# A DMA queue's estimate counts all transfers; a batch's first x + h is put 12 places sooner and cast at once, and block turns wait until its turn is given out

## The chip, the cores and the metric

The kernel runs on one core of a Trainium2 chip. The metric is the device time of one execution in microseconds (us). A core has TensorE (PE, matmuls, with weight loads shown as PEld), VectorE (DVE), ScalarE (ACT), GpSimd (POOL) and SyncE (SP). Here SyncE issues every transfer, in one order; SPq in a row of the trace is that queue.

## The reference

Eight batches, 3136 positions, width 256. An attention without a softmax gates u; its result goes through a mixer of low rank and a two-layer channel part. All inputs and the output are float32.

```python
scores = scale * np.matmul(z, z.transpose(0, 2, 1))      # z: 8 x 3136 x 64, scale = 1 / 3136
attn = np.maximum(scores, 0.0) ** 2
x = u * np.matmul(attn, v)                               # u, v: 8 x 3136 x 256
h = x.transpose(0, 2, 1) @ U @ V                         # U: 3136 x 32, V: 32 x 3136
y = x + h.transpose(0, 2, 1)
ch = np.maximum(y @ w_ch1, 0.0) @ w_ch2                  # 256 -> 1024 -> 256
out = y + ch
```

## The kernel before, in words

**Tiles and stages.** The positions of a batch are cut into 7 groups: six of 512 (groups 0 to 5, four tiles of 128 each) and a last one of 64 (group 6). One pair (batch, group) is an item, and the 56 items are worked off one after the other. During item t the kernel runs the attention-value product (AV) of item t, makes scores for coming items, and finishes the mixer and the channel part of items 7 and 8 places back, that is, of the batch before. All operands of matmuls are bfloat16. Matmuls mostly come in pairs that use the upper and the lower 64 rows of the array at once (`pair`, line 159, whose matmul is line 164; most rows of PE in the trace have that line).

**Blocks.** The score matrix of a batch is symmetric. A block `blk` holds the scores of 512 keys by 512 positions after scale, ReLU (lines 321 and 325) and square (line 315). Where block (J, g) is made and (g, J) is wanted too, it is not computed again: `issue_turn` (line 336) turns it with a DMA transpose on SyncE (line 341) into another block. There are 112 such block turns, and 20 blocks to hold everything. `take_block` and `give_block` hand blocks out first come, first served. A turn becomes ready 7 units after its square; it is then appended to `ready_turns`. The block it reads can't be given back before it is issued.

**The chain from x to ch1.** `av_out` (line 588) writes x = u * AV as bfloat16 (`x_bf`, line 592). When all groups of a batch are there, `t1_all` (line 630) multiplies with U on PE, and DVE finishes the small result `t_sb` (lines 648 and 649). For each group, `u2_unit` (line 661) multiplies V with `t_sb` in four matmuls (rows `ps<-t_sb,V_bf`), and DVE adds x (line 708) into `out_sb` in float32. A cast (`cast`, line 181; rows of line 186 on DVE or 184 on ACT) writes it over `x_bf`, and `x_turn` (line 621) turns it with a DMA transpose (line 624) into `u2T`. The first matmuls of `ch1_part` (line 753) read `u2T`; `ch2_stream` and `ch2_out` make the output. This document calls the result of `u2_unit` "x + h" and the transfer of line 624 the "x turn".

**What sets the order.** The order of all instructions is written out by the Python program ahead of time, with an estimated clock. `clock[0]` counts the matmuls given out so far, in units of a pair's 256 columns (`pe`, line 121). `free_at` holds for ACT, DVE and SP the estimated time at which each is free; `book` (line 102) adds a cost. `hold(due, f)` puts off a step until the clock reaches its due time, and `run_held` (line 109) runs what is due, and then issues ready block turns as long as SP is free by the estimate. In the kernel before, the only entry for SP is 34 units for each block turn (line 345): loads, outputs, x turns and turns of z are not counted.

`emit` (line 857) walks along a light stream (AV or ch2, one unit a place) and puts the other units in at given places: each queue entry is (place, PSUM buffers needed, whether the way of the AV rows turns, unit). An entry that needs a buffer waits up to 14 places beyond its own, or 4 for entries that turn the way in some items, until one is free by the estimate (`ps_ready`, line 171). The x + h of an item's batch before is put in at line 1179.

**Waits on the chip.** SyncE's instructions run in the listed order; each waits for the semaphores of its source, of its target's last readers and of earlier transfers. What is listed behind a waiting transfer waits with it.

Of the kernel before, what the change touches and what calls it, by code (L numbers as in the profile page):

```python
# [18 lines left out]
def kernel(  # L19
# [11 lines left out]
    nc = tc.nc  # L31
# [5 lines left out]
    P = 128  # L37
# [60 lines left out]
    held = []  # L98
    unturned = {}
    ready_turns = []  # L100

    def book(eng, ready, cost):
        free_at[eng] = max(free_at[eng], ready) + cost
        return free_at[eng]

    def hold(due, f):
        held.append((due, len(held), f))

    def run_held(now=None):
        now = clock[0] if now is None else now  # L110
        while True:
            ripe = [h for h in held if h[0] <= now]
            if not ripe:
                break
            h = min(ripe, key=lambda e: (e[0], e[1]))
            held.remove(h)
            h[2]()
        while ready_turns and free_at["sp"] <= now:
            issue_turn(min(ready_turns, key=lambda e: (e[0], e[2], e[1])))

    def pe(cost):
# [75 lines left out]
    def load_tail(raw, c0, a, n):  # L197

        for h in range(2):
            nc.sync.dma_start(out=raw[h * TAIL : (h + 1) * TAIL, c0 : c0 + n], in_=a[NF * P : S, :])  # L200


    def load_z_piece(b, t0, n, raw, tail=True):
        m = min(n, NF - t0)
        nc.sync.dma_start(  # L205
            out=raw[:, : m * dqk].rearrange("p (t d) -> p t d", d=dqk), in_=rows_of(z[b])[:, t0 : t0 + m, :]
        )
        if n > m and tail:
            load_tail(raw, m * dqk, z[b], dqk)
            load_tail(raw, n * dqk, v[b], D)  # L210
# [15 lines left out]
    def load_v_piece(b, k, raw):  # L226
        nc.sync.dma_start(
            out=raw.rearrange("p (t d) -> p t d", d=D), in_=rows_of(v[b])[:, k * GT : (k + 1) * GT, :]
        )

    def v_copy(b, k, raw, copy):
        copy(out=v_bfs[b][:, k * GT : (k + 1) * GT, :], in_=raw.rearrange("p (t d) -> p t d", d=D))
# [41 lines left out]
    def load_u(b, g):  # L274
        g0, gw = groups[g]
        t = pool.tile([P, GT, D], FP32, name="u_sb", bufs=2)
        if gw >= P:
            nc.sync.dma_start(
                out=t[:, : gw // P, :],
                in_=rows_of(u[b])[:, g0 // P : (g0 + gw) // P, :],  # L280
            )
        else:
            nc.sync.dma_start(out=t[:gw, 0, :], in_=u[b, g0 : g0 + gw, :])
        u_sbs[b, g] = t


    def z_turn_dma(b):
        nc.sync.dma_start_transpose(
            out=zzTs[b], in_=z_bfs[b].rearrange("p t c d -> p (t c d)")
        )  # L290

    def z_turn(b, t0, copy):
        n = min(2 * GT, NT - t0)
# [327 lines left out]
    def x_turn(b, g, turned):  # L621
        n = len(tiles_of(g))
        rows = min(P, groups[g][1])
        nc.sync.dma_start_transpose(
            out=turned[:, :n, :, :rows].rearrange("p q d c -> p (q d) c"),
            in_=xs[b, g][:rows, :n, :].rearrange("p q d -> p (q d)"),
        )


    def t1_all(b):  # L630
# [30 lines left out]
    def u2_unit(b, g, turn=True):  # L661
        ts = tiles_of(g)
        n, t0, rows = len(ts), ts[0][1], ts[0][2]
        k, ps = take_ps()
        if n == GT:
            for a in range(2):
                pair(
                    k,
                    crossed(
                        0,  # L670
                        a,
                        lambda h, q: dict(
                            out=four(ps)[:, q, :],
                            lhsT=V4_bf[h, (t0 + q) * P : (t0 + q + 1) * P],
                            rhs=t1s[b][h, :],
                            start=(a == 0),
                            stop=(a == 1),
                        ),
                    ),
                    D,  # L680
                )
        else:
            pair(
                k,
                [
                    (
                        0,
                        0,
                        dict(
                            out=ps[:, 0, :D],  # L690
                            lhsT=V4_bf[:hp, t0 * P : (t0 + 1) * P],
                            rhs=t1s[b][:hp, :],
                            start=True,
                            stop=True,
                        ),
                    )
                ],
                D,
            )
        x = xs[b, g][:rows, :n, :]  # L700
        if b == B - 1:
            entry, raw = stage_block()
            o_blocks[b, g] = entry
            o = raw.rearrange("p (q d) -> p q d", d=D)
        else:
            o = pool.tile([P, GT, D], FP32, name="out_sb", bufs=3)
        done = ps_free[k] = book("dve", clock[0] + 3, 11.2 * n / GT)
        nc.vector.tensor_tensor(out=o[:rows, :n, :], in0=four(ps)[:rows, :n, :], in1=x, op=ALU.add)  # L708
        u2s[b, g] = o
        if not turn:  # L710
            return

        def turned():
            u2Ts[b, g] = u2T_tile()
            x_turn(b, g, u2Ts[b, g])

        def down():
            hold(cast(x, o[:rows, :n, :], n * D) + 2, turned)

        hold(done - 3, down)  # L720


    def u2T_unit(b, g):
# [99 lines left out]
    def ch2_out(b, g, acc):  # L823

        for e in relus.pop((b, g)):
            give_block(e)
        ts = tiles_of(g)
        n, t0, rows = len(ts), ts[0][1], ts[0][2]
        o = u2s.pop((b, g))[:rows, :n, :]
        nc.vector.tensor_tensor(out=o, in0=acc, in1=o, op=ALU.add)  # L830
        dst = rows_of(out[b])[:, t0 : t0 + n, :] if rows == P else out[b, t0 * P : S, None, :]
        nc.sync.dma_start(out=dst, in_=o)
        if (b, g) in o_blocks:
            give_block(o_blocks.pop((b, g)))

# [80 lines left out]
    def load_U():  # L916
        entry, raw = stage_block()
        nc.sync.dma_start(out=raw[:, : NF * R].rearrange("p (t r) -> p t r", r=R), in_=rows_of(moe_U))
        nc.sync.dma_start(out=raw[:TAIL, NF * R : NT * R], in_=moe_U[NF * P :, :])

        def casts():
            cast(U_bf[:, :NF, :], raw[:, : NF * R].rearrange("p (t r) -> p t r", r=R), NF * R)
            cast(U_bf[:TAIL, NF, :], raw[:TAIL, NF * R : NT * R], 100)
            give_block(entry)

        return [casts]

    def load_w(k):
        def step(i):
            entry, raw = stage_block()  # L930
            if k == 0:
                nc.sync.dma_start(out=raw, in_=moe_w_ch1[i * P : (i + 1) * P, :])
                dst = w1_bf[:, i, :]
            else:
                nc.sync.dma_start(
                    out=raw.rearrange("p (t d) -> p t d", d=D),
                    in_=moe_w_ch2.rearrange("(t p) d -> p t d", p=P)[:, i * GT : (i + 1) * GT, :],
                )
                dst = w2_bf[:, i * GT : (i + 1) * GT, :].rearrange("p t d -> p (t d)")

            def casts(entry=entry, raw=raw, dst=dst):
                cast(dst, raw, GT * D)
                give_block(entry)

            return [casts]

        return [lambda i=i: step(i) for i in range(2)]


    def load_V(i0):  # L950
        n = P // 4

        def step(i):
            entry, raw = stage_block()
            w = n * NF + (S - NF * P if i == 3 else 0)
            for c in range(NREP):
                nc.sync.dma_start(out=raw[c * R : (c + 1) * R, :w], in_=moe_V[:, i * n * NF : i * n * NF + w])

            def casts(i=i, entry=entry, raw=raw):
                cast(  # L960
                    V4_bf[:, : NF * P].rearrange("r (t p) -> r t p", p=P)[:, :, i * n : (i + 1) * n],
                    raw[:, : n * NF].rearrange("r (p t) -> r t p", t=NF),
                    2 * n * NF,
                )
                if i == 3:
                    nc.vector.memset(V4_bf[:, S:], 0.0)
                    cast(V4_bf[:, NF * P : S], raw[:, n * NF : n * NF + S - NF * P], 100)
                give_block(entry)

            return [casts]  # L970

        return [lambda i=i: step(i) for i in range(i0, i0 + 2)]
# [110 lines left out]
    for t in range(n_items):  # L1083
# [92 lines left out]
        if av and u2i:  # L1176
            if u2i[1] == 0:
                qm.append((8, 1, False, lambda: t1_all(u2i[0])))
            qm.append((34 if u2i[1] == 0 else 40, 1, False, lambda: u2_unit(*u2i)))

        if not av:
            qm += [(nC // 2, -1, False, small)] if nC else []
# [70 lines left out]
```

## Time and profile before

| what | value |
|---|---|
| median of 3 runs | 1010.28 us (1007.97 to 1010.57) |
| the profiled execution | 1010.08 us |
| its span, from the first to the last instruction | 1008.3 us |
| mean granted TensorE clock | 0.997 |
| DMA queue of SyncE | 165.59 MB, 76.3% of 16 engines' span |
| x turns (line 624) / block turns (line 341) / turns of z (line 288) | 56 / 112 / 7 |

How to read it: a row of the timeline has start and duration in us, engine, line, operation, out<-in, shapes and count; in brackets stands the idle time of the engine before it and who ended it. Rows of one engine that follow each other are merged. In a table of stretches each engine has its busy time and its number of instructions; then come the granted clock of TensorE (1.00 is full speed), the share of the DMA engines that is busy, and GB/s. Matmuls overlap, so the distance between starts tells their pace, not the duration of one.

### The profile page before, as it was taken

Reading aid. Unit: us, or ns where it says so; the run is one execution under the profiler, and the core shown is the slowest. Engines: PE = TensorE matmul, PEld = TensorE weight load, DVE = VectorE, ACT = ScalarE, POOL = GpSimd, SP = SyncE. Lnnn points to the kernel's source line nnn. Section 1 sums busy time; section 2 is a strip of 40 time slices with the busy share of each in tenths; the row PEclk is TensorE's granted clock in tenths of the full one; section 3 lists DMA queues with packets and bytes.
Section 4 is the critical chain, followed back from the end, with each engine's and each line's share of the span. In section 5 each row is a group of like instructions: output and inputs, shape, how many; then the busy total and the mean of one; then the engine's idle time right before and its main releaser. Section 6 shows DMA issues by size and latency. Waiting matters only on the chain.

```text
span 1008.3 us, 35337 instructions
## 1 busy us (share of the span) xinstructions
PE 986.7 (98%) x16179; PEld 784.7 (78%) x16179; DVE 653.6 (65%) x820; ACT 520.2 (52%) x599; POOL 17.2 (2%) x24
## 2 busy tenths in 40 slices
PE   6999899999999999999999999999999999999997
PEld 3898688877787777778777877778777777787776
DVE  5986675668666685666756677566776667653453
ACT  6896653357524573355733456444653356522453
POOL 4100000000000000000000000000000000000000
PEclk9999899999999999999999999999999999999999
DMA  7997998478966799568995789846798577873142
GB/s 247 187 257 178 235 170 166 130 166 186 213 142 165 152 199 218 149 145 181 182 209 157 129 193 188 210 127 140 179 216 185 137 158 143 160 127 88 45 103 94
DMA packets 337061, 167.84 MB, mean 166 GB/s; under 512 B 312336, under 2 KB 315408, under 8 KB 336912
## 3 DMA queue, kind: packets, MB, share of 16 engines
q1 hardware_dynamic: 336912, 165.59, 76.3%
q8 instruction: 126, 2.06, 0.8%
q14 instruction: 23, 0.19, 0.1%
HBM read 62.56 MB, written 25.69 MB: 88 GB/s over the span
## 4 chain that ended last, share of the span: by engine, by line
PE 94%; DVE 2%; ACT 2%; DMA 1%; issue 0%; POOL 0%; SPq 0%; POOLq 0%; ACTq 0%
PE ps L164 92%; PE ps L559 1%; DVE blk L315 1%; ACT blk L793 1%; PE ps L635 1%; DMA blk<-in_v_dram 1%; ACT blk L325 1%; PE ps L843 0%; DMA u2T<-x_bf 0%; DMA stage<-in_v_dram 0%; POOL z_bf L213 0%; SPq L205 0%; DVE blk L321 0%; DVE out_sb L708 0%; DVE blk L830 0%
## 5 line engine op out<-in xcount | busy, mean ns | idle before, releaser
L164 PEld LDWEIGHTS <-blk 64*128 64x128 bf16 x12288 | 617.6, 94 | 153.6 <-POOLq L154 8.7
L164 PE MATMUL ps<-v_bf,blk 64*128 64x256 bf16 x9216 | 617.2, 270 | 2.3 <-DVE blk L315 1.8
L325 ACT ACTIVATE blk<-ps 128x1024 bf16<-128x1024 f32 x324 | 323.4, 1027 | 337.2 <-PE ps L164 334.0
L315 DVE TENSOR_TENSOR blk<-blk 128x1024 bf16<-128x1024 bf16 x352 | 237.7, 701 | 34.1 <-ACT blk L325 33.4
L164 PE MATMUL ps<-u2T,w_bf 64*128 64x512 bf16 (+1 forms) x1792 | 239.1, 351 | 4.3 <-DMA u2T<-x_bf 3.5
L164 PE MATMUL ps<-w_bf,blk 64*128 64x256 bf16 x3072 | 193.7, 269 | 0.2
L790 DVE TENSOR_SCALAR blk<-ps 128x1024 bf16<-128x1024 f32 x96 | 115.7, 1205 | 102.3 <-PE ps L164 102.3
L793 ACT ACTIVATE blk<-ps 128x1024 bf16<-128x1024 f32 (+1 forms) x128 | 107.3, 847 | 82.4 <-PE ps L164 74.1
L164 PE MATMUL ps<-zzT 64*128 64x512 bf16 (+1 forms) x944 | 143.5, 342 | 1.9 <-ACT zzT L305 1.7
L164 PEld LDWEIGHTS <-w_bf 64*128 64x128 bf16 x1792 | 91.6, 94 | 35.1 <-DMA u2T<-x_bf 3.8
L592 DVE TENSOR_TENSOR x_bf<-ps,u_sb 128x1024 bf16<-128x1024 f32 x48 | 58.8, 1224 | 63.0 <-PE ps L164 62.9
L708 DVE TENSOR_TENSOR out_sb<-ps,x_bf 128x1024 f32<-128x1024 f32 (+1 forms) x49 | 54.3, 1107 | 53.7 <-PE ps L164 53.6
L830 DVE TENSOR_TENSOR out_sb<-ps,out_sb 128x1024 f32<-128x1024 f32 x42 | 51.3, 1222 | 18.3 <-PE ps L164 18.3
L164 PEld LDWEIGHTS <-zzT 64*128 64x128 bf16 x944 | 43.9, 95 | 9.2 <-ACT zzT L305 2.2
L325 ACT ACTIVATE last_sb<-ps 128x1024 bf16<-128x1024 f32 x23 | 23.5, 1024 | 26.5 <-PE ps L164 26.5
L321 DVE TENSOR_SCALAR blk<-ps 128x1024 bf16<-128x1024 f32 x24 | 29.4, 1224 | 10.3 <-PE ps L164 8.7
L186 DVE CAST x_bf<-out_sb 128x1024 bf16<-128x1024 f32 x33 | 22.8, 690 | 0.5
L186 DVE CAST v_bf<-stage 128x1024 bf16<-128x1024 f32 (+1 forms) x34 | 21.2, 626 | 0.0
L164 PE MATMUL ps<-t_sb,V_bf 64*128 64x256 bf16 x200 | 20.8, 269 | 0.0
L164 PE MATMUL ps<-v_bf,last_sb 64*128 64x256 bf16 x192 | 18.6, 269 | 0.0
L830 DVE TENSOR_TENSOR blk<-ps,blk 128x1024 f32<-128x1024 f32 x6 | 7.3, 1225 | 16.0 <-PE ps L164 15.9
L578 ACT COPY u_sb<-ps 64x512 f32<-64x512 f32 x8 | 4.7, 582 | 23.9 <-PE ps L559 23.9
(67 smaller groups left out, 249.5 us busy)
## 6 DMA issues: line engine op xcount, KB each, us to landing
u_sb<-in_u_dram SPq DMA_DIRECT2D x48, 512.0 KB, 5.0
stage<-in_v_dram SPq DMA_DIRECT2D x42, 512.0 KB, 6.0
out_dram<-out_sb SPq DMA_DIRECT2D x42, 512.0 KB, 3.1
stage<-in_z_dram SPq DMA_DIRECT2D x7, 512.0 KB, 5.5
blk<-in_v_dram SPq DMA_DIRECT2D x6, 512.0 KB, 7.2
out_dram<-blk SPq DMA_DIRECT2D x6, 512.0 KB, 2.6
blk<-in_moe_w_ch_dram SPq DMA_DIRECT2D x4, 512.0 KB, 5.8
stage<-in_z_dram SPq DMA_DIRECT2D x7, 256.0 KB, 5.7
```

Source lines behind the costliest of these rows:

```text
L164: ins = nc.tensor.matmul(**args)
L186: nc.vector.tensor_copy(out=out, in_=in_)
L315: nc.vector.tensor_tensor(out=a, in0=a, in1=a, op=ALU.mult)
L321: nc.vector.tensor_scalar(out=dst, in0=src, scalar1=scale, scalar2=0.0, op0=ALU.mult, op1=ALU.max)
L325: nc.scalar.activation(out=dst, in_=src, func=AF.Relu, scale=scale)
L559: nc.tensor.matmul(out=ps[c * hp : c * hp + rows, h, :D], lhsT=smalls[b][h * hp : (h + 1) * hp, jt, :], rhs=v_bfs[b][h * hp : (h + 1) * hp ...
L592: nc.vector.tensor_tensor(out=xs[b, g][:rows, :n, :], in0=four(box["ps"])[:rows, :n, :], in1=u_sbs[b, g][:rows, :n, :], op=ALU.mult,)
L635: nc.tensor.matmul(out=pt[c * R : (c + 1) * R, 0, :D], lhsT=U_bf[:rows, it, :], rhs=xs[b, g][:rows, q, :], start=(it < NREP), stop=(it + N ...
L708: nc.vector.tensor_tensor(out=o[:rows, :n, :], in0=four(ps)[:rows, :n, :], in1=x, op=ALU.add)
L790: nc.vector.tensor_single_scalar(out=r, in_=ps[:, :, :gw], scalar=0.0, op=ALU.max)
L793: nc.scalar.activation(out=r, in_=ps[:, :, :gw], func=AF.Relu)
L830: nc.vector.tensor_tensor(out=o, in0=acc, in1=o, op=ALU.add)
```

## The change

Four edits. First, a new function `queued` books SP's estimated time for every transfer by its size in KB: 15 units for 512 KB of plain transfer, 17 for 256 KB of an x turn or a turn of z. It is called behind each load, output, x turn and turn of z. The 34 units of a block turn stay. Second, `u2_unit` of a batch's first group (g == 0) does the cast on DVE at once behind the add, and holds the x turn until 6 units before the estimated end of that cast. Third, from that `u2_unit` until its x turn is given out, the list `urgent` is not empty, and `run_held` issues no ready block turn. Fourth, that `u2_unit` is due at place 22 of its item, not 34. (A block turn that AV needs at once would still be issued from `av_stream`; that code is not changed.)

```diff
+    urgent = []
...
+    def queued(kb, turned=False):
+
+        book("sp", clock[0], kb * (17 / 256 if turned else 15 / 512))
...
-        while ready_turns and free_at["sp"] <= now:
+        while ready_turns and free_at["sp"] <= now and not urgent:
             issue_turn(min(ready_turns, key=lambda e: (e[0], e[2], e[1])))
...
@@ load_tail, load_z_piece, load_v_piece, load_u, z_turn_dma, x_turn, ch2_out, load_U, load_w, load_V
+            queued(n / 4)                      (each of two small loads of the tail)
+        queued(m * dqk / 2)                    (z)
+        queued(GT * D / 2)                     (v; w_ch1, w_ch2)
+        queued(gw)                             (u)
+        queued(NT * P / 4, True)               (turn of z)
+        queued(n * D / 4, True)                (x turn)
+        queued(n * rows)                       (output)
+        queued(NF * R / 2)                     (U)
+                queued(w / 8)                  (each of four loads of V)
...
@@ u2_unit
         def turned():
             u2Ts[b, g] = u2T_tile()
             x_turn(b, g, u2Ts[b, g])
+            urgent.clear()
 
         def down():
             hold(cast(x, o[:rows, :n, :], n * D) + 2, turned)
 
-        hold(done - 3, down)
+        if g == 0:
+            urgent.append((b, g))
+            nc.vector.tensor_copy(out=x, in_=o[:rows, :n, :])
+            hold(book("dve", done, 6.3) - 6, turned)
+        else:
+            hold(done - 3, down)
...
-            qm.append((34 if u2i[1] == 0 else 40, 1, False, lambda: u2_unit(*u2i)))
+            qm.append((22 if u2i[1] == 0 else 40, 1, False, lambda: u2_unit(*u2i)))
```

More of the change, by code (lines that the diff above doesn't have):

```diff
@@ L200, in load_tail @@
             nc.sync.dma_start(out=raw[h * TAIL : (h + 1) * TAIL, c0 : c0 + n], in_=a[NF * P : S, :])
+            queued(n / 4)
     def load_z_piece(b, t0, n, raw, tail=True):
@@ L207, in load_z_piece @@
         )
+        queued(m * dqk / 2)
         if n > m and tail:
@@ L229, in load_v_piece @@
         )
+        queued(GT * D / 2)
     def v_copy(b, k, raw, copy):
@@ L283, in load_u @@
             nc.sync.dma_start(out=t[:gw, 0, :], in_=u[b, g0 : g0 + gw, :])
+        queued(gw)
         u_sbs[b, g] = t
@@ L290, in z_turn_dma @@
         )
+        queued(NT * P / 4, True)
     def z_turn(b, t0, copy):
@@ L627, in x_turn @@
         )
+        queued(n * D / 4, True)
     def t1_all(b):
@@ L832, in ch2_out @@
         nc.sync.dma_start(out=dst, in_=o)
+        queued(n * rows)
         if (b, g) in o_blocks:
@@ L919, in load_U @@
         nc.sync.dma_start(out=raw[:TAIL, NF * R : NT * R], in_=moe_U[NF * P :, :])
+        queued(NF * R / 2)
         def casts():
@@ L939, in step @@
                 dst = w2_bf[:, i * GT : (i + 1) * GT, :].rearrange("p t d -> p (t d)")
+            queued(GT * D / 2)
             def casts(entry=entry, raw=raw, dst=dst):
@@ L957, in step @@
                 nc.sync.dma_start(out=raw[c * R : (c + 1) * R, :w], in_=moe_V[:, i * n * NF : i * n * NF + w])
+                queued(w / 8)
             def casts(i=i, entry=entry, raw=raw):
```

## The prediction

> **What bounds the kernel now.** First the page of the profiled execution: its span, the engines' shares and the chain that ended last.
>
> ```profile
> span 1008.3 us, 35337 instructions
> PE 986.7 (98%) x16179; PEld 784.7 (78%) x16179; DVE 653.6 (65%) x820; ACT 520.2 (52%) x599; POOL 17.2 (2%) x24
> PE 94%; DVE 2%; ACT 2%; DMA 1%; issue 0%; POOL 0%; SPq 0%; POOLq 0%; ACTq 0%
> ```
>
> TensorE (PE) is the bound: it is busy 98% of the span and the chain runs through it for 94%. Only its idle time can be saved without taking matmuls out, and the change takes none out. So next comes the view of who waited for whom, for PE alone, over the whole span, and then the same view from 130 to 940 us.
>
> ```profile
> PE ps L296 <- ACT z_bf L213: 4.1, 1, 4.1
> PE ps L164 <- DMA u2T<-x_bf: 3.5, 1, 3.5
> PE ps L296 <- POOL z_bf L213: 3.4, 1, 3.4
> PE ps L164 <- DVE blk L315: 1.8, 2, 0.9
> ```
> ```profile
> PE ps L164 <- DVE out_sb L708: 0.2, 1, 0.2
> ```
>
> In the long middle, where six of the eight batches lie, PE waits 0.2 us in all: nothing can be won there. The waits on z_bf belong to the first 12 us, whose order is not touched. One wait touches the change: a single 3.5 us for `u2T`, the turned x + h. The timeline of PE places it in batch 0, at the first up-projection (ch1) of the whole kernel.
>
> ```profile
> 113.24 0.94 PE L164 MATMUL ps<-v_bf,blk 64*128 64x256 bf16 x14
> 114.01 0.40 PE L164 MATMUL ps<-v_bf,last_sb 64*128 64x256 bf16 x4
> 114.22 0.62 PE L164 MATMUL ps<-v_bf,blk 64*128 64x256 bf16 x8
> 118.38 1.04 PE L164 MATMUL ps<-u2T,w_bf 64*128 64x512 bf16 x4 [3.54 <-DMA u2T<-x_bf]
> ...
> 120.70 1.92 PE L164 MATMUL ps<-v_bf,blk 64*128 64x256 bf16 x16
> 122.41 0.64 PE L164 MATMUL ps<-zzT 64*128 64x512 bf16 x2
> ...
> 124.57 0.59 PE L164 MATMUL ps<-u2T,w_bf 64*128 64x512 bf16 x4
> ```
>
> The stall has a second part. Before it, 14 matmuls of 256 columns take 114.01 - 113.24 = 0.77 us, 0.055 us each; after it, 16 of the same kind take 122.41 - 120.70 = 1.71 us, 0.107 us each. The table of stretches says why, by its column PEclk (0.50, then 1.00):
>
> ```profile
> 118.30:124.40 6.10, 6.02 (x46) 3.43 (x48) 0.46 (x1) 3.27 (x4) 0.00 (x0) 0.50 1.01 254
> 124.40:130.00 5.60, 5.60 (x88) 4.10 (x85) 5.25 (x7) 3.79 (x6) 0.00 (x0) 1.00 1.11 163
> ```
>
> Behind the stall TensorE ran at half clock for some 6 us. Why u2T is late is seen on SyncE's queue (SP), which issues every transfer in order, beside VectorE (DVE), which makes what it turns:
>
> ```profile
> 105.26 2.76 SPq L341 DMA_TRANSPOSE blk<-blk  x1
> 108.06 1.05 SPq L278 DMA_DIRECT2D u_sb<-in_u_dram  x2
> 109.22 4.64 SPq L341 DMA_TRANSPOSE blk<-blk  x1
> 113.96 1.25 SPq L624 DMA_TRANSPOSE u2T<-x_bf  x1
> 115.32 3.35 SPq L341 DMA_TRANSPOSE blk<-blk  x1
> ```
> ```profile
> 102.61 0.22 DVE L649 COPY t_sb<-t_sb 64x256 bf16<-64x256 bf16 x1
> ...
> 103.48 0.69 DVE L315 TENSOR_TENSOR last_sb<-last_sb 128x1024 bf16<-128x1024 bf16 x1
> 104.08 1.29 DVE L315 TENSOR_TENSOR blk<-blk 128x1024 bf16<-128x1024 bf16 x2
> 105.47 1.22 DVE L708 TENSOR_TENSOR out_sb<-ps,x_bf 128x1024 f32<-128x1024 f32 x1
> 106.61 1.28 DVE L315 TENSOR_TENSOR blk<-blk 128x1024 bf16<-128x1024 bf16 x2
> 107.81 0.69 DVE L186 CAST x_bf<-out_sb 128x1024 bf16<-128x1024 f32 x1
> ```
>
> The cast was done at 107.81 + 0.69 = 108.5 us, but the turn was issued at 113.96: 5.5 us behind a queue in which two block turns held SP for 2.76 and 4.64 us.
>
> **The change part by part.** *The u2 unit sooner.* In the order in which the changed program lists its instructions, the x + h of batch 0's first group stands 22 matmuls sooner; in batches 1 to 6 it stands at the very same matmul as before, since the unit waits there for a free PSUM buffer whichever of the two places it is due at. In batch 0 it comes two matmuls into the first of these rows, instead of at the second:
>
> ```profile
> 103.63 1.25 PE L164 MATMUL ps<-v_bf,blk 64*128 64x256 bf16 x20
> ...
> 105.05 0.38 PE L164 MATMUL ps<-t_sb,V_bf 64*128 64x256 bf16 x4
> ```
>
> That is 103.63 + 2 x 0.055 = 103.74 us, 1.3 us sooner. Its operand t_sb is ready at 102.61 + 0.22 = 102.83, so the new place adds no wait. DVE still has squares queued; one fewer stands ahead of the add, so at their pace (0.6 us) the add L708 starts near 104.9 rather than 105.47.
>
> *The cast at once.* The add lasts 1.22 us and the cast 0.69: ready near 106.7, not 108.5. The two squares that stood between them come later. They are of scores whose turns are held back anyway, and no row shows PE waiting for a square in the window from 130 to 940 us. Without that cover a delay of 0.7 us is the most that one cast can put before a square. I take zero and keep 0 to 0.7 for each of seven batches, 0 to 5 us in all, with most of it near zero, since DVE is idle 35% of the span.
>
> *The fuller estimate and the turns held back.* No instruction is added: 112 block turns and 56 x + h turns remain, in another order. In the changed order, both block turns between the z loads and this x turn (the rows of 2.76 and 4.64 us) stand behind it, and there are three fewer in all since the w_ch2 loads. What stands ahead is the u loads (1.05 us), which follow PE's place and end near 107. So the x turn goes out at about 107. How long does it take to land? These are the view of u2T and the page's list of issues:
>
> ```profile
> DMA to landing us min/median/max: 2.3/3.3/5.4
> ```
> ```profile
> blk<-blk SPq DMA_TRANSPOSE x112, 5.2
> ```
>
> It lands between 107 + 3.3 = 110.3 and 107 + 5.4 = 112.4. ch1 needs it where the 8 matmuls from 114.22 end, 114.22 + 8 x 0.055 = 114.66. The margin is 2.3 to 4.4 us; at 118.38 it was nought. The stall is gone whole.
>
> What is late next: the block turns that step back. In the changed order, the smallest distance from a block turn's place to the matmul that reads it is 222 matmuls, 13 us by this run's clock (batch 0, block 5 for group 3), against 5.2 us for a turn to land; in batches 2 to 7 it is 25 us. No buffer is asked for sooner, and a turn takes its target block later, so more blocks are free. The next x turn, group 1 in each batch, has little margin. For batch 1 these rows show the queue, the landing and its reader:
>
> ```profile
> 247.47 9.99 SPq L341 DMA_TRANSPOSE blk<-blk  x3
> 257.55 1.47 SPq L624 DMA_TRANSPOSE u2T<-x_bf  x1
> ```
> ```profile
> DMA to landing us min/median/max: 4.9/4.9/4.9
> ```
> ```profile
> 263.16 0.59 PE L164 MATMUL ps<-u2T,w_bf 64*128 64x512 bf16 x4
> ```
>
> It lands at 262.5, 0.7 us before 263.16. Three block turns (9.99 us) stood ahead of it; in the changed order there are two. The margin grows by up to 3.3 us rather than shrinking.
>
> *The sum.* Stall: 118.38 - 114.66 = 3.7 us. Half clock: from 118.38 to 124.57 is 6.19 us, of which 1 - 0.055/0.107 = 0.49 is lost, 3.0 us; with the last 0.4 us already at full pace I take 2.9. Together 6.6 us. The profiled execution lasted 1010.08 us (span 1008.3 and 1.8 around it), so 1010.08 - 6.6 = 1003.5; that execution is 0.2 us under the median of the runs, 1010.28. I say 1003.6.
>
> The half clock may be weighed against a rule. The Trainium skill (TensorE: Matmul & The Clock Gate, section "What's actually happening") says that the clock falls to half after an idle window of about 3.4 us, and that this window runs freely. The row at 0.50 behind a 3.54 us wait agrees. By that rule the half clock is a matter of phase, and a run of the old kernel that escapes it would be 2.9 us shorter: the gain would then be 3.7 us, with the same new time.
>
> **The rivals.** *Only part of the stall goes* (6%). If the x turn still finds SP behind a slow transfer and lands 1 to 3 us past 114.66, that much stall stays. For it: SP was busy without a break around 109 us. Against it: the two transfers that blocked it stand behind it now. A wait of 3.41 us at the start left the clock whole, as PEclk 1.00 in the second row shows:
>
> ```profile
> 11.58 1.04 PE L296 MATMUL ps<-ident,z_bf 128*128 128x128 bf16 x8 [3.41 <-POOL z_bf L213]
> ```
> ```profile
> 0.00:25.20 25.20, 15.13 (x173) 9.54 (x175) 14.35 (x14) 15.23 (x17) 12.39 (x19) 1.00 0.77 247
> ```
>
> So the half clock would not come with a shorter stall: 1004.6 to 1006.6.
>
> *The forced cast and the new order of DVE cost PE short waits* (8%): 0.3 to 0.7 us in each of seven batches, 1005.6 to 1008.4. Against it: 0.2 us of such waits in 810 us now.
>
> *The change does not do what it says* (4%): in batches 1 to 6 the earlier place indeed changes nothing. If in batch 0 the wait only moves to the u loads or the add, 3.5 us and the half clock stay: 1010.
>
> *Held turns come late together* (4%, slower). They now fall between later x turns, once a batch, where group 3's x turn had none ahead of it. Each such stall is paid in six batches, so from 6.6/6 = 1.1 us of lateness a batch the gain is eaten; at 3.5 us with the half clock it is 6 x 6.4 - 6.6 = 32 us, 1042. Against it stand these rows of batch 1:
>
> ```profile
> 291.25 1.25 SPq L624 DMA_TRANSPOSE u2T<-x_bf  x1
> ```
> ```profile
> 301.26 0.59 PE L164 MATMUL ps<-u2T,w_bf 64*128 64x512 bf16 x4
> ```
>
> It has 10 us from issue to reader; with one block turn ahead (up to 4.64 us above) and 5.4 to land it still fits.
>
> **How the numbers follow.** The forecast, stall gone and no new one, has the remaining 78% and a range of its own of 1002 to 1005. About 0.3%, 3 us, is what a measurement here can tell from no change: faster means under 1007.2. Forecast, partial stall and most of the short waits lie there: 0.78 + 0.06 + 0.04 = 0.88, of which I give 0.03 back for what I have not seen: 0.85. Within 0.3%: the rest of the short waits and the case of no effect, 0.09. Slower: the last rival and as much for the unseen, 0.06. The range must leave out no more than 0.2: downward 1.8 us below the forecast, since the runs before spread by 2.6 us; upward to 1007.0, which takes in the partial stall and the middle of the short waits.
>
> **What would show it.** Right: PE's waits have no line on u2T, PEclk is 1.00 in every stretch from 98 to 240 us, the x turn L624 of batch 0 (its line number shifts) is issued near 107 us and the batches keep their period. Wrong: a wait on u2T or on a turned block at any place, a stretch at 0.50, or PE waits on DVE after 130 us that sum to more than 1 us.

## The result and the profile after

| kernel | median us | runs | ratio to the kernel before |
|---|---|---|---|
| before | 1010.57 | 1007.97 to 1011.47 (5) | 1 |
| changed | 1004.9 | 1002.38 to 1005.57 (5) | 0.9943, 95% interval 0.9923 to 0.9962 |

The change makes the kernel faster by 0.57%. The profiled execution of the changed kernel took 1002.76 us, with a span of 1001.0 us. Lines have shifted: the pair's matmul is line 169 now, the x turn 634, a block turn 351, the add of x + h 719, the cast at once 734. First the view of who PE waited for, over the whole span (us in total, times, longest):

```profile
PE ps L306 <- ACT z_bf L220: 4.1, 1, 4.1
PE ps L169 <- DVE blk L325: 2.8, 4, 0.9
PE ps L169 <- ACT zzT L315: 1.7, 2, 1.1
PE ps L169 <- DVE v_bf L191: 0.5, 1, 0.5
PE ps L861 <- ACT blk L810: 0.4, 1, 0.4
PE ps L306 <- POOL z_bf L220: 0.2, 1, 0.2
```

The wait for u2T is gone. The queue of SyncE around the first x turn, in the changed kernel's timeline:

```profile
98.35 1.11 SPq L205 DMA_DIRECT2D stage<-in_z_dram  x2
99.51 1.23 SPq L205 DMA_DIRECT2D stage<-in_v_dram  x2
100.84 1.00 SPq L286 DMA_DIRECT2D u_sb<-in_u_dram  x2
105.19 1.26 SPq L634 DMA_TRANSPOSE u2T<-x_bf  x1
106.99 1.82 SPq L351 DMA_TRANSPOSE blk<-blk  x1
```
```profile
104.47 0.69 DVE L734 CAST x_bf<-out_sb 128x1024 bf16<-128x1024 f32 x1
```

SyncE is idle from 101.8 to 105.2 and issues the x turn as soon as the cast is done, at 104.47 + 0.69 = 105.16; before, it was busy without a break up to 119 us. On PE, the same eight matmuls as before lead to the first ch1, and a later row can be matched too, since both timelines have 48 matmuls in between:

```profile
112.69 0.62 PE L169 MATMUL ps<-v_bf,blk 64*128 64x256 bf16 x8
113.13 0.61 PE L169 MATMUL ps<-u2T,w_bf 64*128 64x512 bf16 x4
...
116.39 0.61 PE L169 MATMUL ps<-u2T,w_bf 64*128 64x512 bf16 x4
```

The lead on the kernel before is 114.22 - 112.69 = 1.53 us ahead of ch1 and 124.57 - 116.39 = 8.18 us behind the place of the old half clock: 6.65 us were won there, and nothing else lies between. No stretch ran at half clock (the column before the last two):

```profile
108.00:130.00 22.00, 21.54 (x341) 18.48 (x339) 16.60 (x24) 16.40 (x18) 0.00 (x0) 1.00 0.97 163
130.00:240.00 110.00, 109.91 (x1837) 93.03 (x1833) 72.09 (x91) 52.41 (x62) 0.00 (x0) 1.00 0.85 181
```

But the whole span is only 7.3 us shorter. The chain shows what was given back. Two batches of the kernel before and then of the changed one (start, duration, count of matmuls in that piece):

```profile
239.71 90.68 PE ps L164 x1464
361.37 90.68 PE ps L164 x1464
```
```profile
243.75 78.35 PE ps L169 x1270
365.66 78.35 PE ps L169 x1270
```

A batch took 361.37 - 239.71 = 121.66 us and now takes 365.66 - 243.75 = 121.91: 0.25 us more, and that in five batches. The timeline says where: the scores behind the second x + h of a batch now wait for its PSUM buffer, which DVE's add frees at 242.47 + 1.23 = 243.70 us.

```profile
242.47 1.23 DVE L719 TENSOR_TENSOR out_sb<-ps,x_bf 128x1024 f32<-128x1024 f32 x1
...
242.91 0.71 PE L169 MATMUL ps<-v_bf,blk 64*128 64x256 bf16 x10
...
243.75 0.39 PE L169 MATMUL ps<-zzT 64*128 64x512 bf16 x2
```

Of the lead of 8.18 us, five times 0.25 or 1.3 us are lost again, which leaves 6.9. The other 0.4 us of the 7.3 were won at the second x + h of batch 0: the kernel before waits 0.2 us there for the same kind of buffer (the line on `out_sb` in its view of waits), and the changed kernel, whose second x + h stands six matmuls sooner, doesn't.

The lead of 1.5 us at 112 us has nothing to do with the change: it stems from the first 12 us, where PE's wait for GpSimd's z_bf was 3.4 us in the profile of before and 0.2 here, in code that is the same. A second profile of the changed kernel (below) has 3.3 us there again.

### The profile page after: what moved, and what is told of

Its sections match the earlier page's. It is cut to its first block, busy times and chain, and to the rows that moved or that the text cites. A ratio compares the mean times of both kernels' runs of the same rounds, so it can differ in the third digit from the quotient of the medians.

```text
span 1001.0 us, 35345 instructions
## 1 busy us (share of the span) xinstructions
PE 984.9 (98%) x16179; PEld 820.1 (82%) x16179; DVE 655.9 (66%) x822; ACT 520.3 (52%) x597; POOL 16.6 (2%) x24
## 4 chain that ended last, share of the span: by engine, by line
PE 94%; DVE 3%; ACT 2%; issue 0%; DMA 0%; POOLq 0%; ACTq 0%
PE ps L169 92%; DVE blk L325 1%; PE ps L569 1%; ACT blk L810 1%; PE ps L646 1%; DVE out_sb L719 1%; ACT blk L335 1%; PE ps L861 0%; DMA blk<-in_z_dram 0%; DVE blk L331 0%; DVE blk L847 0%; DVE blk L1065 0%; DVE x_bf L602 0%; PE ps L306 0%; ACT zzT L315 0%
## 5 line engine op out<-in xcount | busy, mean ns | idle before, releaser
L169 PEld LDWEIGHTS <-blk 64*128 64x128 bf16 x12288 | 647.6, 94 | 123.6 <-POOLq L159 8.7
L335 ACT ACTIVATE blk<-ps 128x1024 bf16<-128x1024 f32 x334 | 333.1, 1027 | 330.3 <-PE ps L169 328.5
L807 DVE TENSOR_SCALAR blk<-ps 128x1024 bf16<-128x1024 f32 (+1 forms) x114 | 132.1, 1159 | 96.1 <-PE ps L169 95.2
L810 ACT ACTIVATE blk<-ps 128x1024 bf16<-128x1024 f32 (+1 forms) x110 | 93.4, 859 | 82.7 <-PE ps L169 75.2
L169 PEld LDWEIGHTS <-w_bf 64*128 64x128 bf16 x1792 | 95.8, 94 | 27.4 <-POOLq L159 3.0
L169 PEld LDWEIGHTS <-zzT 64*128 64x128 bf16 x944 | 46.1, 95 | 8.4 <-issue 2.6
L331 DVE TENSOR_SCALAR blk<-ps 128x1024 bf16<-128x1024 f32 x14 | 17.1, 1224 | 5.6 <-PE ps L169 4.8
L191 DVE CAST x_bf<-out_sb 128x1024 bf16<-128x1024 f32 x28 | 19.3, 690 | 0.5
```

Source lines behind the costliest of these rows:

```text
L169: ins = nc.tensor.matmul(**args)
L191: nc.vector.tensor_copy(out=out, in_=in_)
L331: nc.vector.tensor_scalar(out=dst, in0=src, scalar1=scale, scalar2=0.0, op0=ALU.mult, op1=ALU.max)
L335: nc.scalar.activation(out=dst, in_=src, func=AF.Relu, scale=scale)
L807: nc.vector.tensor_single_scalar(out=r, in_=ps[:, :, :gw], scalar=0.0, op=ALU.max)
L810: nc.scalar.activation(out=r, in_=ps[:, :, :gw], func=AF.Relu)
```

## The experiments

All times are medians; "before" was run on the same chip with each set (1009.57, 1009.64 and 1009.13 us). The theories: **Q**, that the x turn was late for its place in SyncE's queue, behind two block turns; **M**, that x + h itself was made late; later **E**, that the DMA engines' backlog decides.

### One edit at a time, put into the kernel before

**Place 22 alone.**

```diff
-            qm.append((34 if u2i[1] == 0 else 40, 1, False, lambda: u2_unit(*u2i)))
+            qm.append((22 if u2i[1] == 0 else 40, 1, False, lambda: u2_unit(*u2i)))
```

> The kernel before with the fourth edit alone (place 22). The first x + h stands 22 matmuls sooner, but the two block turns of 2.76 and 4.64 us are still listed ahead of its x turn. Theory Q (the queue made it late): the x turn still goes out at 113 to 114 us, PE still waits 3 to 3.7 us for u2T, and the time stays within 1 us of before, near 1010. Rival M (x + h itself was made late): the x turn goes out 1.3 us sooner, the wait falls to about 2.2 us, the half clock goes, and the time is near 1006.

1007.42 us (1005.04 to 1011.02), ratio 0.9987, interval 0.9971 to 1.0002: no difference that this measurement can tell from none. Its queue:

```profile
107.51 1.05 SPq L278 DMA_DIRECT2D u_sb<-in_u_dram  x2
108.66 4.91 SPq L341 DMA_TRANSPOSE blk<-blk  x1
113.67 1.25 SPq L624 DMA_TRANSPOSE u2T<-x_bf  x1
```

The x turn went out at 113.67, as Q expects and M does not. But the median is 2.2 us below the kernel before, where Q allowed 1. PE came to ch1 1 us later than otherwise, since a cast of v_bf had moved to ACT (a wait of 1.5 us, where the kernel before waits 0.5 for DVE), so its wait for u2T was 2.5 us, and it was not followed by the half clock in the profiled run:

```profile
118.07 0.61 PE L164 MATMUL ps<-u2T,w_bf 64*128 64x512 bf16 x4 [2.53 <-DMA u2T<-x_bf]
```

The ten runs fall into two groups by their mean granted clock: the five up to 1006.84 us have 0.999 or 1.000, the five from 1008.0 on 0.997 or 0.998. (A half-clock stretch of 3.41 us takes 0.0017 off the mean.) Of the 53 runs of the kernel before in the three sets, 52 have 0.998 or less. So the half clock seems to spare about half of the runs where the wait is a microsecond shorter, which would explain the lower median; only one run was profiled.

**The cast at once alone**, for all seven batches.

```diff
-        hold(done - 3, down)
+        if g == 0:
+            nc.vector.tensor_copy(out=x, in_=o[:rows, :n, :])
+            hold(book("dve", done, 6.3) - 6, turned)
+        else:
+            hold(done - 3, down)
```

> The kernel before with the cast at once alone (second edit, all seven batches; nothing held back). The two block turns are still ahead. Q: x turn at 113 to 114 us, wait of 3 to 3.7 us, near 1010; by the decomposition of the changed kernel the short waits of 0.25 us in each of five batches are there too, since they came with this edit: up to 1011. M: the cast ends 1.2 us sooner, wait about 2.3 us without the half clock, near 1006.

1011.1 us (1008.94 to 1012.76), ratio 1.0016, interval 1.0004 to 1.0027: slightly slower. The wait for u2T was 3.8 us; M falls. The chain of this run, two batches:

```profile
251.79 78.35 PE ps L164 x1270
373.74 78.35 PE ps L164 x1270
```

373.74 - 251.79 = 121.95 us a batch: this edit by itself brings the 0.25 us and more.

**The hold-back alone.**

```diff
+    urgent = []
-        while ready_turns and free_at["sp"] <= now:
+        while ready_turns and free_at["sp"] <= now and not urgent:
+            urgent.clear()                    # in turned(), behind x_turn
+        if g == 0:
+            urgent.append((b, g))
         hold(done - 3, down)
```

> The kernel before with the hold-back alone (third edit). The 4.64 us block turn moves behind the x turn, the 2.76 us one stays ahead; x + h and its cast are as before (cast done at 108.5). Q: the x turn goes out near 109 us and lands at 112.5 to 114.6, before ch1 needs it at 114.7: no wait, no half clock, near 1003.6. M: no change, 1010.

1006.46 us, with runs from 1002.01 to 1009.56; ratio 0.9966, interval 0.9946 to 0.9986. Half of what Q expected in the median, and both ends in the runs. The profiled run is one of the longer (1008.56 us): its queue, the landing of its x turn and its PE.

```profile
105.98 3.24 SPq L342 DMA_TRANSPOSE blk<-blk  x1
109.27 1.05 SPq L279 DMA_DIRECT2D u_sb<-in_u_dram  x2
110.42 1.24 SPq L625 DMA_TRANSPOSE u2T<-x_bf  x1
```
```profile
DMA to landing us min/median/max: 7.5/7.5/7.5
```
```profile
118.00 0.61 PE L165 MATMUL ps<-u2T,w_bf 64*128 64x512 bf16 x4 [2.49 <-DMA u2T<-x_bf]
```
```profile
118.00:119.20 1.20, 1.20 (x16) 0.79 (x18) 0.00 (x0) 0.00 (x0) 0.00 (x0) 1.00 1.28 287
119.20:122.60 3.40, 3.40 (x30) 1.92 (x28) 0.21 (x1) 3.02 (x4) 0.00 (x0) 0.51 1.11 230
```

The x turn went out 3.5 us sooner than in the kernel before (Q expected it near 109, and the u loads held it up to 110.4), but needed 7.5 us to land (110.42 to 117.95), more than any of the 56 x turns of the kernel before (5.4 at most). So Q is not the whole of it. And PE fell to half clock for 3.4 us behind a wait of 2.49 us, 1.2 us after it had gone on. The runs show the same split: the four up to 1004.35 us have a mean granted clock of 1.000, the six from 1005.98 on 0.998.

**The fuller estimate alone**: all calls of `queued`, and nothing else of the change.

> The kernel before with the fuller estimate alone (first edit). One block turn is still listed right ahead of the x turn, but three fewer turns stand in the queue before it. Q: that one turn starts when its square is done, near 107.5, holds SP for 2.8 to 4.6 us, and the x turn goes out at 110.5 to 112 and lands at 114 to 116: a wait of 0 to 1.5 us, no half clock, 1003.6 to 1005. M: no change, 1010. If the fuller estimate costs PE short waits in the long middle, the gain of PE on the kernel before shrinks from batch to batch here; my theory is that it does not.

1004.42 us (1003.88 to 1005.24), ratio 0.9944, interval 0.9926 to 0.9962: the gain of the whole change, from one edit. Its queue and the landing of its x turn:

```profile
103.42 1.01 SPq L286 DMA_DIRECT2D u_sb<-in_u_dram  x2
109.26 1.91 SPq L351 DMA_TRANSPOSE blk<-blk  x1
111.26 1.71 SPq L634 DMA_TRANSPOSE u2T<-x_bf  x1
```
```profile
DMA to landing us min/median/max: 5.1/5.1/5.1
```

Two block turns fewer ahead (10 before the u loads, not 12; three fewer had been expected) let the u loads go out at 103.4 instead of 108.1. The block turn ahead of the x turn now holds SyncE for 1.91 us and not for 4.64. The wait for u2T is 0.3 us. A batch takes 121.66 us as before, so this edit costs the long middle nothing.

### What decides when the x turn lands

**A u load behind the x turn.** To the hold-back alone, one load is moved:

```diff
-            hold(clock[0] + 60, lambda t=t: load_u(*items[t + 1]))
+            hold(clock[0] + (125 if t == NG else 60), lambda t=t: load_u(*items[t + 1]))
```

> The hold-back alone again, but u of batch 1, group 1 (512 KB) is loaded behind the first x turn instead of ahead of it. With the hold-back alone the x turn went out at 110.4 and landed only at 117.95, 7.5 us later, behind two u loads that landed at 114.0 and 115.3. Theory E (the DMA engines' backlog decides, not the place in SyncE's queue): the load costs SyncE only 0.4 us to issue, yet the x turn lands about 2 us sooner, near 115.5 to 116, and PE's wait of 2.5 us falls below 1. Rival Q (the place in SyncE's queue decides): issue and landing move by 0.5 us only and the wait stays at 2 us or more.

1003.65 us (1003.29 to 1004.79), ratio 0.9946, interval 0.9925 to 0.9967.

```profile
105.57 3.07 SPq L342 DMA_TRANSPOSE blk<-blk  x1
108.69 0.57 SPq L279 DMA_DIRECT2D u_sb<-in_u_dram  x1
109.36 1.24 SPq L625 DMA_TRANSPOSE u2T<-x_bf  x1
```
```profile
DMA to landing us min/median/max: 4.6/4.6/4.6
```

Issued 1.1 us sooner than with the hold-back alone, the x turn lands 4.0 us sooner (at 113.97, not 117.95), and PE has no wait for it; all four runs have a mean granted clock of 0.999 or 1.000. A transfer of 512 KB ahead of it costs SyncE half a microsecond and the x turn 2.9 us on the engines: E. It was expected to land at 115.5; the size was underestimated.

**The change without the fuller estimate.**

```diff
     def queued(kb, turned=False):
-        book("sp", clock[0], kb * (17 / 256 if turned else 15 / 512))
+        return
```

> The changed kernel without the fuller estimate (first edit): place 22, cast at once and hold-back remain. The x turn still has the 2.76 us block turn, two more turns and both u loads shortly before it. E: it goes out near 108.5, when SyncE is through with the u loads, and lands near 116 behind them: a wait of about 1 to 2 us on PE, sometimes with the half clock, 1005 to 1008, and with the short waits of the cast edit. Q: nothing that blocks SyncE stands between the cast and the x turn any more, so it lands within 5.4 us, by 114: no wait, 1004.

1006.25 us, with runs from 1002.29 to 1010.66; ratio 0.9976, interval 0.9956 to 0.9996. The profiled run is the shortest: its x turn went out at 106.96 and landed 5.6 us later, at 112.54, with ch1 at 112.67, a margin of 0.1 us, where the changed kernel has 4.7 (108.40 against 113.13). Both theories missed it in part; the spread of 8 us in the runs, against 3 in the changed kernel, fits a transfer that lands just before or just after its reader, but the longer runs were not profiled. Their granted clock is on record: it is 0.997 or 0.998 in the four runs from 1009.44 us on, and 0.999 or 1.000 in the five up to 1004.96, as a stretch at half clock in the long ones would make it.

**The change without the cast at once**: the hold stays, `hold(done - 3, down)` is back for all groups.

> The changed kernel without the cast at once (second edit): estimate, hold-back and place 22 remain. In the changed kernel PE loses 0.25 us on the kernel before in each of five batches, where the scores behind the second x + h wait for its PSUM buffer. Theory C: this comes from the cast's booking on DVE. Then the loss is gone here, the lead of 7 us over the kernel before that PE has at 130 us stays to the end, and the time is 1.2 us below that of the changed kernel from the same start, 1003 to 1003.7. Rival: it comes from the estimate or the place; then the loss of 0.25 us a batch remains.

1002.01 us (1001.6 to 1004.11), ratio 0.9932, interval 0.9909 to 0.9955. Two batches of its chain:

```profile
231.38 90.68 PE ps L169 x1464
353.01 90.68 PE ps L169 x1464
```

353.01 - 231.38 = 121.63 us: the loss of 0.25 us a batch is gone. The cast edit alone had brought it; taken out, it goes. (The run without the fuller estimate, which has the cast, keeps a batch of 121.91 us.) The x turn still landed at 108.24, 5 us ahead of ch1, so this edit wasn't needed for it. The interval of the time overlaps that of the changed kernel; it is the chain that shows the loss and its end.

### The start, and the favoured edits together

**The same, with another order on GpSimd at the start.**

```diff
-    cast_v(0, on_pool)
     cast_z(1, 0, on_pool)
     cast_z(1, 1, on_pool)
+    cast_v(0, on_pool)
```

> The same, with one more move at the start: GpSimd casts the second piece of z before the first piece of v, not behind it. Theory S: runs of one kernel spread by 2.6 us since the first v piece lands at 6 us in some and at 8.5 in others, and GpSimd, waiting for it, holds back the z that PE needs (waits of 0.2 to 4.0 us in the profiles). Then PE's wait for GpSimd is under 0.5 us here in any run, the runs lie within 1 us of each other, and the median is 1 to 2 us lower. Rival: the v piece is needed right after by the AV, so the wait only changes its name, and median and spread stay.

1001.86 us (1001.17 to 1002.83). PE's wait for GpSimd is gone from the view of waits, the spread is 1.7 us instead of 2.5, and the median is 0.15 us lower. A median 1 to 2 us lower and runs within 1 us of each other had been expected, and neither came: with four runs each, this doesn't settle what the order is worth.

**The changed kernel again**, unchanged, beside the next two.

> The changed kernel itself, beside the next two on one chip: 1002 to 1006, again spread by the start; no wait for u2T; a loss of 0.25 us in each of five batches.

1004.0 us (1001.77 to 1004.78), ratio 0.9938, interval 0.992 to 0.9956. In its profile (1004.78 us) PE waited 3.3 us for GpSimd's z_bf at the start, in that of the first profile (1002.76 us) 0.2.

**The kernel before with that order at the start alone.**

> The kernel before with GpSimd's casts reordered at the start alone (z before v). Theory S: PE's wait of 3.4 us for GpSimd shrinks under 0.5 us, PE is 1.5 to 2.4 us ahead at its 100th matmul, and the wait for u2T stays: 1007 to 1008.5. Rival (the wait for the v piece only changes its name): within 0.5 us of before.

1007.79 us (1004.06 to 1008.77), ratio 0.9985, interval 0.997 to 1.0, which just reaches no difference. PE was 2.4 us ahead by its 100th matmul, and then lost part of it at the very same place:

```profile
111.83 0.62 PE L164 MATMUL ps<-v_bf,blk 64*128 64x256 bf16 x8
116.96 1.04 PE L164 MATMUL ps<-u2T,w_bf 64*128 64x512 bf16 x4 [4.52 <-DMA u2T<-x_bf]
```

It came to ch1 2.4 us sooner (111.83 against 114.22), but u2T let it go on only 1.4 us sooner (116.96 against 118.38): a wait for a transfer swallows a microsecond won upstream of it.

**What the runs favour, put together**: the fuller estimate and the hold-back, place 34 and the old cast, the u load behind the x turn, and the new order at the start.

> What the runs favour put together: the fuller estimate and the hold-back, x + h at its old place with its old cast, u of batch 1, group 1 loaded behind the first x turn, and z before v on GpSimd at the start. The x turn goes out near 107 to 108 and lands by 113, before ch1: no wait for u2T, no half clock, no loss in the long middle, no wait of 1.5 us for v_bf (that came with place 22). Start 2.3 us and u2T 6.5 us off the 1010: 1001.0 to 1001.8, below the changed kernel by 2 to 4 us. If theory S falls, it is near 1002.5 with the old spread.

1001.47 us (1001.41 to 1002.09), ratio 0.9921, interval 0.99 to 0.9942. The x turn:

```profile
100.90 0.54 SPq L286 DMA_DIRECT2D u_sb<-in_u_dram  x1
107.34 1.24 SPq L634 DMA_TRANSPOSE u2T<-x_bf  x1
```
```profile
DMA to landing us min/median/max: 3.3/3.3/3.3
```

It lands at 110.6, 2.9 us ahead of ch1, no wait for v_bf of 1.5 us is left, and a batch takes 121.63 us. Its median is 2.5 us below that of the changed kernel on the same chip, and its four runs lie within 0.7 us; its interval and that of the changed kernel overlap.

## Why the prediction was right

It said 1003.6 us, and the median is 1004.9. By its own steps:

- **Where the gain is.** Right. The one stall on u2T and the half clock behind it were given 3.7 + 2.9 = 6.6 us; the matched rows measure 6.65. A further 0.4 us was won right behind it, at the second x + h of batch 0, and nothing in the long middle.
- **The u2 unit sooner.** Its 1.3 us are there, and that it changes nothing in batches 1 to 6 held. But alone it gains nothing that can be told, and the edits put together last do without it. That it adds no wait was wrong in one point: with the old cast, it moves a cast of v_bf to ACT, and PE waits 1.5 us for that.
- **The x turn at about 107, landing by 110.3 to 112.4.** Measured 105.19 and 108.40 in a run whose start was 1.5 us early; 107.19 and 110.24 in the second profile. Right in size, but not by the step given. The prediction had the x turn follow the u loads, which were to end near 107; they were issued by 101.8, and it was the cast, done at 105.16, that the x turn waited for. That the two came to the same 107 is luck. The reason given for the delay before was half of it, too: the prediction put it on two block turns that held SyncE. The hold-back alone took the 4.64 us turn out of the way and the x turn still landed at 117.95, right behind u loads of 1 MB; with one of these loads behind it, it took 2.9 us less. The 3.3 to 5.4 us taken for the landing don't hold there. The fuller estimate sees to that: two of the four block turns in the 20 us before the x turn are gone from there, the u loads go out sooner, and the engines' busy share is 0.73 from 106 to 112 us, where the kernel before has 1.06 from 108 to 114.
- **The cast at once, taken at zero.** This is the term that was mis-sized: it costs 0.25 us in each of five batches, 1.3 us in all, within the bounds of 0 to 5 that were kept. The prediction looked for squares that come later; what came later was a PSUM buffer. In the changed order the second x + h of these batches stands four matmuls later, and the scores behind it get its buffer before DVE has emptied it. That it moves because the cast changes what the planner books on DVE is read from the program; no run isolates it. The rival of short waits named the kind and the place on DVE, with 0.3 to 0.7 us in each of seven batches, which is more than it was. One of the prediction's own signs of being wrong is met here: PE waits on DVE behind 130 us of more than 1 us in sum. The view of waits has no line for them, as each is short; the chain has all five.
- **What is late next: nothing.** Right. In the long middle PE waits for no transfer, and the x turn of batch 1, group 1 goes out at 247.16 and lands 4.3 us ahead of its reader, where it had 0.7.
- **A shorter stall leaves the clock whole.** Wrong, and the row that it rested on was misread. The clock's record in that trace begins only at 15.12 us, and a table of stretches gives 1.00 for what has no record. PE's rows behind the wait of 3.41 us at the start show half pace:

```profile
12.55 1.89 PE L164 MATMUL ps<-v_bf,blk 64*128 64x256 bf16 x16
14.23 1.04 PE L164 MATMUL ps<-zzT 64*128 64x512 bf16 x4
15.08 1.06 PE L164 MATMUL ps<-v_bf,blk 64*128 64x256 bf16 x16
15.98 0.59 PE L164 MATMUL ps<-zzT 64*128 64x512 bf16 x4
```

The first 16 matmuls take 14.23 - 12.55 = 1.68 us, 0.105 each; as many from 15.08 on take 0.90 us, 0.056 each. So nothing at the start spoke for a whole clock behind a short wait. Behind 2.49 us in the run with the hold-back alone, the clock fell to half; behind 2.53 us in the profiled run with place 22 it didn't. The part of the cited rule that fits both is a window that runs freely: the low stretches last 3.41 us (with the hold-back alone and with the cast alone) or 6.83 (in the kernel before, with and without the new order at the start), one or two windows of the Trainium skill's 3.4 us (TensorE: Matmul & The Clock Gate, section "What's actually happening"). In the hold-back run the clock's record begins at 16.84 us and the fall comes at 119.23, 102.4 us or 30 such windows later. The window that ends there, from 115.82 on, holds 2.2 us of the wait. In the run with place 22 the record begins at 14.66; 30 windows later, at 117.06, a boundary cuts the wait into 1.5 and 1.0 us. The other part of the rule, an idle window of about 3.4 us, doesn't fit: 2.2 us idle in a window were enough, and the measurement decides. This is worked out from one profile of each run, and no run was made to test it.
- **The slower rival**, held turns that come late together, didn't occur: every block turn lands at least 12 us ahead of its reader in the changed kernel.

The start moves single runs by 1 to 2 us either way, so that the closeness of 1003.6 and 1004.9 proves little by itself. With the start taken out, the two profiles of the changed kernel agree: the first is 1.5 us ahead of the kernel before at the eight matmuls that lead to ch1 and 7.3 at the end; the second is 0.5 us behind there (114.69 against 114.22) and 5.3 ahead at the end (spans of 1003.0 and 1008.3). Both gain 5.8 us, where 6.6 were forecast: 6.65 at the stall and 0.4 behind it, less 1.3 for the cast.

## What to carry to other kernels

A stall of a few microseconds on one transfer can be worth nearly twice its length, where the matmul clock falls behind it (3.7 and 2.9 us here); look at the granted clock after each wait, and at the matmuls' pace where the clock has no record. When a transfer is late, ask for its issue and its landing separately: a place further ahead in the queue helps only as far as the engines are not still busy with what was issued before. And an edit made for one stall should be put in only where that stall is: the cast at once, applied to all batches, cost 1.3 us and wasn't needed in the first.

## What was not expected of the hardware

An x turn of 256 KB, which lands in 3.3 us in the median of the kernel before, took 7.5 us behind two loads of 512 KB that SyncE had issued in 1.05 us. A block turn held SyncE's queue for 4.64 us with the engines' busy share at 1.06 (108 to 114 us of the kernel before) and for 1.91 us with it at 0.69 (the same stretch with the fuller estimate), so a queue that looks busy may only be showing the engines' backlog. And TensorE's clock fell to half behind a wait of 2.49 us, after 1.2 us of full-speed matmuls, and stayed whole behind one of 2.53 us.
